# A recurrence and its feed-forward block on one core: units of single instructions, and a new order on every engine

## The chip, the cores and the metric

The kernel runs on 1 core of one Trainium2 chip. Its time is the device time of one execution, in microseconds (us). The kernel before takes 648.21 us (median of 3 runs, 648.15 to 649.47). The engines are TensorE (PE, with its weight loads as PEld), VectorE (DVE), ScalarE (ACT), GpSimd (POOL) and SyncE (SP), which issues most DMAs.

## What is computed

```python
# q, k, v, a_re, a_im: batch 4, heads 8, 768 steps, head size 48, fp32
mag = np.sqrt(a_re * a_re + a_im * a_im)
scale = np.minimum(mag, 0.999) / (mag + 1e-06)
a_re_n, a_im_n = (a_re * scale, a_im * scale)
for t in range(S):
    new_re = ar * S_re - ai * S_im
    new_im = ar * S_im + ai * S_re
    S_re, S_im = (new_re + kv, new_im)         # kv = outer product of k[t], v[t]
    y[:, :, t] = np.einsum('bhd,bhde->bhe', q[:, :, t], S_re)
x = y.transpose(0, 2, 1, 3).reshape(3072, 384)
h = np.maximum(x @ w_in, 0.0)                  # w_in 384 x 2048, given in float64
out = (h * h @ w_out).astype(np.float32)       # w_out 2048 x 384
```

## The kernel before

The sequence is cut into 24 chunks of 128 steps, and the chunks into 12 groups of 2 (`GC`). For each group a set of **operands** is made on DVE and ACT from the raw gates, queries and keys (`make_operands`, line 784): squares, an inverse root in two stages, the limit on the gates' size, products of the gates along 8-step blocks (`steps_in_blocks`, seven steps of a product and a sum), running **totals** over the blocks (`totals`, line 912, fifteen small instructions on line 918), the totals carried back into the blocks (`carries`, `carried`), and four products with queries and keys into the tile `qk`. The fourth head of each pair is copied by a DMA into the tile `last`. The first two groups (`BY_CHUNK`) are made in two halves each, chunk by chunk; the plan calls them p and q (`p0`, `q0`, `p1`, `q1`), later whole groups `o`.

Each chunk (`chunk`; `a` and `b` are the two of a group) then makes on PE its products with the state before it and its scores (both in `scores`), the transposed keys (`turns`), the values summed by the masked scores (`y`, line 1059), and the new state. `tokens` copies y into `x` on ACT, and `fill_gaps` (`g`, line 1129) fills the rest of x with two DMAs. The FFN block of a group is `first_product` (`F`, PSUM tile `h_ps`), ReLU and square on ACT (`H`), and the second product: plain for the first two groups (`T`), later with sums and differences of halves on DVE (`X`, `Y`, `Q`) that save one product in eight (`Z`, outputs `R`).

The weights arrive as 64-bit words and are decoded: two ACT instructions (`U`, `S`) and one on DVE (`A`) for each of 16 blocks. Each weight is read again later and watched on ACT (`w` loads, `W` is two ACT instructions, lines 704 and 705). At the end a range count (`K0` on DVE, `K1` one matmul, `K2` a cast) says whether the fast path held; every engine loads it (line 1456) and branches (line 1457).

No scheduler decides the order. A long string, `FRONT`, lists units in an order written out by hand, and every engine's instructions, its DMA issues too, follow that order:

```python
    by_hand = {mybir.EngineType.DVE, mybir.EngineType.PE, mybir.EngineType.SP,
               mybir.EngineType.Activation, mybir.EngineType.Pool}
    with tc.manual_schedule(engines=by_hand):
        follow(FRONT)
```

`keep_busy` (`I`) puts two filler matmuls on the identity matrix into the order (line 579, tile `idle`).

Of the kernel before, what the change touches and what calls it, by code (L numbers as in the profile page):

```python
# [33 lines left out]
P = 128  # L34
HH = 2
# [394 lines left out]
def quotient_path(ctx, tc, feat, vtok, w_in, w_out, w1, w2, out, n_seq, count):  # L430
# [77 lines left out]
    BY_CHUNK = 2  # L508

# [266 lines left out]
    def four(name="pr"):  # L776

        return tmp.tile([P, 4 * NP * D], F32, tag="pr", name=name)

    products_of = set()  # L780
# [3 lines left out]
    def make_operands(gi, only=None):  # L784
# [8 lines left out]
        tiles = {}  # L793

        def room(pool, shape, name):
            if (gi, name) not in rooms:
                rooms[gi, name] = pool.tile([P, GC // nb * shape[0], *shape[1:]], F32, name=name)
            at = 0 if only is None else only * shape[0]
            return rooms[gi, name][:, at:at + shape[0]]
# [11 lines left out]
        def steps_in_blocks(js):  # L811

            for j in js:
                ab = tiles["ab"]
                pr = four()[:, 0:4 * n].rearrange("p (k c n) -> p k c n", k=2, c=2)

                tt(pr, planes(ab[:, 2:, j - 1], -1, 0), planes(ab[:, :, j], 1, 1), ALU.mult)
                tt(ab[:, now, j], pr[:, 0], pr[:, 1], ALU.add)

        def squares():  # L820
            tiles["room"] = room(nrm, [4, E], "room")
            tiles["sq"], tiles["both"] = tiles["room"][:, 0:2], tiles["room"][:, 2:4]
            nc.scalar.activation(out=tiles["sq"], in_=r[:, A_RE:A_IM + 1], func=AF.Square)

        def real_parts():

            tiles["ab"] = room(prd, [3, L, n], "ab")
            turned(tiles["ab"][:, 1:2], r[:, A_RE:A_IM])

        def imaginary_parts():  # L830
            tiles["ab"] = room(prd, [3, L, n], "ab")
# [8 lines left out]
        def first_inverse():  # L840
            tiles["z"] = room(nrm, [1, E], "z")[:, 0]
# [9 lines left out]

        def inverse():
            u, v, z = tiles["sq"][:, 0], tiles["sq"][:, 1], tiles["z"]
            tt(v, u, v, ALU.mult)
            nc.vector.scalar_tensor_tensor(out=z, in0=v, scalar=3.0, in1=z, op0=ALU.subtract,  # L855
                                           op1=ALU.mult)


# [19 lines left out]
        def gates():  # L878
            f, low, v, ab = (tiles["both"][:, 0], tiles["both"][:, 1], tiles["sq"][:, 1],
                             tiles["ab"])  # L880
            nc.vector.scalar_tensor_tensor(out=f, in0=f, scalar=1.0, in1=low, op0=ALU.min,
                                           op1=ALU.mult)
            both_parts = ab[:, now].rearrange("p c j n -> p c (j n)")
            tt(both_parts, both_parts, f.unsqueeze(1).to_broadcast([P, 2, E]), ALU.mult)
# [605 lines left out]
```

## Time and profile before

| what | value |
|---|---|
| median of 3 runs | 648.21 us |
| the profiled execution | 651.88 us |
| its span, first to last instruction | 650.1 us |
| mean granted TensorE clock in it | 0.988 |
| PE busy | 616.5 us (95%) |
| PE weight loads busy | 554.6 us (85%) |
| DVE busy | 480.0 us (74%) |
| ACT busy | 430.5 us (66%) |
| POOL busy | 72.0 us (11%) |
| moved by DMA | 60.59 MB, mean 93 GB/s |

The shares are averages over a start, in which weights and operands have to come first, a long middle and a short end. PE's busy time counts filler matmuls too, 25.8 us of them. So the table says which engine is full on the average, and not what a change at either end of the program is worth; for that the views in order of time are needed.

### The profile page before, as it was taken

The page shows a single profiled execution, that of the slowest core. Times are in us where ns is not written, and L with a number is a line of the kernel's source. Part 1 is how long each engine was busy: PE and PEld are TensorE (multiplying, and loading weights), DVE is VectorE, ACT ScalarE, POOL GpSimd, SP SyncE. Part 2 cuts the span into 40 slices and gives each one's busy share as a digit, 9 for nine tenths or more (in the row PEclk, how much of TensorE's full clock was granted, in tenths as well). Part 3 has the DMA queues.
Part 4 walks back from the last instruction along what each step waited for, and adds up shares of the span by engine and source line. Part 5 has one row for each costly group of instructions (what it writes and reads, how often), then busy time and mean ns, then how long its engine had stood idle before and what let it go on. Part 6 is the DMA issues. An engine that isn't in the chain of part 4 may idle for free.

```text
span 650.1 us, 15843 instructions
## 1 busy us (share of the span) xinstructions
PE 616.5 (95%) x6467; PEld 554.6 (85%) x6467; DVE 480.0 (74%) x937; ACT 430.5 (66%) x847; POOL 72.0 (11%) x154
## 2 busy tenths in 40 slices
PE   2679999999999999999999999999999999999994
PEld 2678977677899889889899899999899899889994
DVE  6868887896989877977969678877957958842040
ACT  6758998667677593784686685686695584653430
POOL 7760120010100020000030010001000001000000
PEclk9879999999999999999999999999999999999998
DMA  8988575160640620722554523642541630133101
GB/s 172 178 176 182 170 234 94 40 135 11 113 80 8 123 75 8 132 64 54 112 136 117 89 44 92 114 123 77 102 99 50 93 87 13 57 86 105 49 1 31
DMA packets 41883, 60.59 MB, mean 93 GB/s; under 512 B 6024, under 2 KB 30024, under 8 KB 41800
## 3 DMA queue, kind: packets, MB, share of 16 engines
q1 hardware_dynamic: 39624, 55.46, 39.1%
q0 software_dynamic: 1888, 3.69, 3.3%
q8 instruction: 53, 0.87, 0.6%
q10 hardware_dynamic: 288, 0.32, 0.2%
q14 instruction: 30, 0.25, 0.2%
HBM read 48.76 MB, written 4.72 MB: 82 GB/s over the span
## 4 chain that ended last, share of the span: by engine, by line
PE 83%; DMA 6%; ACT 5%; DVE 2%; POOL 2%; issue 1%; ACTq 0%; POOLq 0%; DVEq 0%
PE h_ps L1153 32%; PE o_ps L1243 28%; PE o_ps L1173 5%; PE a_ps L1022 5%; PE y L1059 3%; PE h_ps L1137 3%; PE y L1005 3%; PE turns L1032 2%; PE turns L1084 2%; DMA raw<-in_feat_dram 2%; DMA words<-in_moe_w_out_dram 1%; DMA last<-qk 1%; DMA x<-x 1%; DMA words<-in_moe_w_in_dram 1%; PE idle L579 1%
## 5 line engine op out<-in xcount | busy, mean ns | idle before, releaser
L1153 PE MATMUL h_ps<-x,w 128*128 128x256 f32 x960 | 212.6, 380 | 0.0
L1153 PEld LDWEIGHTS h_ps<-x,w 128*128 128x128 f32 x960 | 180.9, 190 | 24.2 <-DMA x<-x 0.2
L1243 PE MATMUL o_ps<-w,h 128*128 128x192 f32 x640 | 110.7, 329 | 0.0
L1243 PEld LDWEIGHTS o_ps<-w,h 128*128 128x128 f32 x640 | 103.7, 190 | 1.6 <-ACT o L1116 0.3
L1160 ACT ACTIVATE h<-h_ps 128x512 f32<-128x512 f32 x80 | 47.6, 595 | 75.9 <-PE h_ps L1153 70.3
L1243 PE MATMUL o_ps<-w_sum,mix 128*128 128x192 f32 x320 | 55.9, 330 | 0.7 <-DVE o L1119 0.7
L568 POOL COPY vt<-vt 64x192 f32<-64x192 f32 x48 | 28.2, 588 | 241.2 <-DMA vt<-in_vtok_dram 229.3
L1243 PEld LDWEIGHTS o_ps<-w_sum,mix 128*128 128x128 f32 x320 | 51.7, 190 | 1.7 <-DVE o L1119 1.0
L1161 ACT ACTIVATE h<-h 128x512 f32<-128x512 f32 x80 | 50.5, 631 | 2.6
L499 DVE TENSOR_TENSOR pr<-ab 128x384 f32<-128x384 f32 (+1 forms) x98 | 49.0, 500 | 3.7 <-ACT ab L889 1.3
L499 DVE TENSOR_TENSOR mix<-h 128x256 f32<-128x256 f32 x40 | 16.9, 422 | 41.7 <-ACT h L1161 41.7
L499 DVE TENSOR_TENSOR qk<-ab,qk 128x768 f32<-128x768 f32 (+1 forms) x56 | 46.3, 844 | 1.4
L1137 PE MATMUL h_ps<-x,w 128*128 128x128 f32 x384 | 44.8, 277 | 1.5 <-DMA x<-x 1.5
L499 DVE TENSOR_TENSOR room<-ab,carry 128x1344 f32<-128x1344 f32 (+1 forms) x28 | 36.8, 1354 | 12.5 <-ACT carry L937 11.6
L1137 PEld LDWEIGHTS h_ps<-x,w 128*128 128x128 f32 x384 | 43.6, 192 | 2.5 <-issue 1.6
L1173 PE MATMUL o_ps<-w,h 128*128 128x384 f32 x128 | 44.0, 489 | 1.1 <-ACT o L1116 1.1
L1071 ACT COPY x<-y 64x256 f32<-64x256 f32 (+1 forms) x72 | 26.5, 368 | 20.0 <-PE y L1059 18.9
L808 ACT ACTIVATE ab<-raw 128x768 f32<-128x768 f32 (+1 forms) x28 | 36.8, 1371 | 2.3 <-DVE qk L499 2.3
L1022 PE MATMUL a_ps<-qk 48*64 48x64 f32 (+1 forms) x1152 | 37.6, 245 | 0.0
L579 PE MATMUL idle<-ident 128*128 128x128 f32 x168 | 25.8, 325 | 12.4 <-POOL ident masks.py:199 12.4
L808 ACT ACTIVATE room<-z 128x768 f32<-128x768 f32 (+1 forms) x27 | 36.0, 1392 | 1.6 <-DVE z L855 1.6
L1022 PEld LDWEIGHTS a_ps<-qk 48*64 48x64 f32 x1152 | 36.0, 134 | 0.7 <-issue 0.5
(114 smaller groups left out, 993.2 us busy)
## 6 DMA issues: line engine op xcount, KB each, us to landing
raw<-in_feat_dram SPq DMA_DIRECT2D x40, 288.0 KB
words<-in_moe_w_out_dram SPq DMA_DIRECT2D x8, 768.0 KB
again<-in_moe_w_in_dram SPq DMA_DIRECT2D x16, 384.0 KB
again<-in_moe_w_out_dram SPq DMA_DIRECT2D x16, 384.0 KB
last<-qk SPq DMA_DIRECT2D x48, 97.5 KB
words<-in_moe_w_in_dram SPq DMA_DIRECT2D x8, 576.0 KB
vt<-in_vtok_dram SPq DMA_DIRECT2D x48, 96.0 KB
out_dram<-o SPq DMA_DIRECT2D x23, 192.0 KB
```

Source lines behind the costliest of these rows:

```text
L499: nc.vector.tensor_tensor(out=out, in0=in0, in1=in1, op=op)
L568: nc.gpsimd.tensor_copy(out=v[half_rows(h), PAD + DM:PAD + DM + DM // 2].rearrange("t (a x) -> t a x", x=HH * D), in_=pairs[half_rows(1 - ...
L579: nc.tensor.matmul(idle, lhsT=ident, rhs=ident, start=True, stop=True)
L808: nc.scalar.activation(out=out.rearrange("p c j n -> p c n j"), func=AF.Copy, in_=in_.rearrange("p c (n j) -> p c n j", j=L), **kwargs)
L1022: nc.tensor.matmul(to[:, :, 2] if s else to[:, :, 0:2], lhsT=operand(2 + c, p_, rows(hh))[:, half_rows(s)], rhs=q_[:, :, 1] if s else q_, ...
L1071: nc.scalar.copy(out=x_of[gi][to, odd::2, b * C:(b + 1) * C], in_=tiles["y"][odd][of, 0:NP // 2])
L1137: nc.tensor.matmul(ps[:, j], lhsT=w1_blocks[:, k, g, at:at + P], rhs=x_of[i][:, g, b * C:(b + 1) * C], start=(g == 0), stop=(g == NG - 1))
L1153: nc.tensor.matmul(ps[:, j], lhsT=w1_blocks[:, k, g, at:at + P], rhs=x_of[i][:, g], start=(g == 0), stop=(g == NG - 1))
L1160: nc.scalar.activation(out=h, in_=h_ps[i, f], func=AF.Relu, scale=of_w1)
L1161: nc.scalar.activation(out=h, in_=h, func=AF.Square)
L1173: nc.tensor.matmul(o_of[i, b], lhsT=tokens_of(i, f, b)[:, j], rhs=w2[:, k], start=(k == 0), stop=(k == NFB - 1))
L1243: nc.tensor.matmul(to, lhsT=x(k)[:, j], rhs=factor(z)[:, 2 * k + j], start=(z in (0, 1, 3) and k == j == 0), stop=(k == KH // 2 - 1 and j ...
```

## The change

Units become finer: nearly each is one instruction now (a product, a sum, a copy), so that the plan can order each by itself. The tiles of half groups are laid out so that both halves share one. The totals of the first group go from POOL to DVE. A chunk's products with the state before it become a unit of their own (`sums_of_before`), apart from the scores, and a unit of two POOL memsets (`ordered`) follows them. `FRONT` is written anew for all engines, the filler matmuls are cut from 84 to 36, and the range count has another place in it.

```diff
     BY_CHUNK = 2
+    TOTALS_ON_POOL = set()
...
-    def four(name="pr"):
-
-        return tmp.tile([P, 4 * NP * D], F32, tag="pr", name=name)
+    def two(name="pr"):
+
+        return tmp.tile([P, 2 * NP * D], F32, tag="pr", name=name, bufs=2)
...
-        def steps_in_blocks(js):
-
-            for j in js:
-                ab = tiles["ab"]
-                pr = four()[:, 0:4 * n].rearrange("p (k c n) -> p k c n", k=2, c=2)
-
-                tt(pr, planes(ab[:, 2:, j - 1], -1, 0), planes(ab[:, :, j], 1, 1), ALU.mult)
-                tt(ab[:, now, j], pr[:, 0], pr[:, 1], ALU.add)
+        def step_products(j):
+
+            ab = tiles["ab"]
+            pr = tiles["pr", j] = two()[:, 0:4 * n].rearrange("p (k c n) -> p k c n", k=2, c=2)
+            tt(pr, planes(ab[:, 2:, j - 1], -1, 0), planes(ab[:, :, j], 1, 1), ALU.mult)
+
+        def step_sums(j):
+            pr = tiles["pr", j]
+            tt(tiles["ab"][:, now, j], pr[:, 0], pr[:, 1], ALU.add)
...
         def totals():
-            total = tiles["ab"][:, now, L - 1]
-            eng = nc.gpsimd if only is not None and gi == 0 else nc.vector
-            other_room = tiles["both"].rearrange("p k e -> p (k e)")
+            eng = nc.gpsimd if (gi, only) in TOTALS_ON_POOL else nc.vector
...
+        def sums_of_before():
+
+            ys = sums_here()
+            for pair in range(0, NP, 2):
+                for c in (RE, IM):
+                    for hh in range(HH):
+                        for p_ in (pair, pair + 1):
+                            nc.tensor.matmul(
+                                ys[p_ % 2][crossed(hh, p_), p_ // 2],
+                                lhsT=states[b][1 - c_seq % 2][rows(hh), c, columns(hh, PAD + p_ * D)],
+                                rhs=operand(c, p_, rows(hh)),
+                                start=(p_ < 2 and c == RE), stop=False, skip_group_check=True)
...
+        def ordered():
+
+            nc.gpsimd.memset(states[b][1 - c_seq % 2][:, :, PAD + NP * D:], 0.0)
+            nc.gpsimd.memset(v[:, 0:PAD], 0.0)
...
     FRONT = (
-        "M6 M10 M2 l0.0.0 l0.0.1 M0 j1 p0.0 p0.3 p0.4 p0.5 p0.2 j0 p0.7 i0.1.0 p0.1 p0.8 M3 M4 "
...
-        "Z11.6 K1 K2 s11.2 R11.6 s11.0 s11.1")
+        "M8 M5 l0.0.0 M2 p0.2 M10 l0.0.1 i0.1.0 M9 j1 j3 j0 i0.1.1 p0.1 p0.0 M0 p0.3 p0.4 p0.5 "
...
+        "Z11.6 R11.6 s11.1 W7 K0 K1 K2")
```

Three places of the orders follow. First ACT at the start of the program, before: `sums` is the small activation that needs the table, `room` takes the squares, `z` the first inverse, `ab` the turned copies of the gates.

```order
L590 ACT_TABLE_LOAD
L590 ACTIVATE sums<-tiny 128x1
L823 ACTIVATE room<-raw 128x768
L842 ACTIVATE z<-room 128x384
L846 ACTIVATE room,sums<-z 128x384
L808 ACTIVATE ab<-raw 128x48x8 x2
L808 ACTIVATE room<-z 128x48x8
```

And the same place of the changed kernel:

```order
L818 ACT_TABLE_LOAD
L818 ACTIVATE ab<-raw 128x48x8
L533 DMA raw<-in_feat_dram 48x2x384
L818 ACTIVATE ab<-raw 128x48x8
L832 ACTIVATE room<-raw 128x2x384
L591 ACT_TABLE_LOAD
L591 ACTIVATE sums<-tiny 128x1
L848 ACTIVATE z<-room 128x384
L852 ACTIVATE room,sums<-z 128x384
L832 ACTIVATE room<-raw 128x2x384
L818 ACTIVATE room<-z 128x48x8
L848 ACTIVATE z<-room 128x384
```

The turned copies went ahead of the squares, a second table load stands between the squares and the first inverse, and the second half's squares and first inverse stand among the first half's pieces.

Second, DVE of the changed kernel in the midst of the first group's two halves (`pr<-ab 128x192` is a step's product, `ab<-pr 128x2x48` its sum, L955 the totals, `w_58` the first weights):

```order
L683 SCALAR_TENSOR_TENSOR w_58<-words,part 128x768
L499 TENSOR_TENSOR pr<-ab 128x192
L955 TENSOR_TENSOR pr<-ab 128x96
L499 TENSOR_TENSOR ab<-pr 128x2x48
L955 TENSOR_TENSOR ab<-pr 128x24 x2
L499 TENSOR_TENSOR pr<-ab 128x192
L955 TENSOR_TENSOR pr<-ab 128x48
L499 TENSOR_TENSOR ab<-pr 128x2x48
```

Before, these totals stood on POOL (its line 918), and DVE had the steps of one half without a break; now the totals of one half alternate with the steps of the other.

Third, DVE at the end of the changed kernel (`sums`, `ends`, `sizes` and `good` are the range count; the two L1192 are the last sums of outputs):

```order
L499 TENSOR_TENSOR h<-h 128x2x128
L1192 SCALAR_TENSOR_TENSOR o<-o_ps,o 128x192 x2
L1506 TENSOR_SCALAR sums<-sums 128x14
L1506 TENSOR_SCALAR ends<-ends 128x72
L1506 TENSOR_SCALAR sizes<-sizes 128x32 x2
L1510 TENSOR_REDUCE least<-sums 128x1
L1510 TENSOR_REDUCE least<-ends 128x1
L1510 TENSOR_REDUCE least<-sizes 128x1
L1512 TENSOR_REDUCE good<-least 128x1
L1501 CAST count<-turns 1x1
```

And ACT there, whose last watch (L705, L706) writes `sizes`:

```order
L1189 ACTIVATE o<-o_ps 128x192 x3
L705 ACTIVATE size,sizes<-again 128x384
L706 ACTIVATE size,sizes<-size,bound 128x384
L1583 TENSOR_LOAD count
```

Before, the whole of the count but matmul and cast stood ahead of DVE's last two output sums, and ACT's last watch ahead of its last two output copies; now both stand behind them.

## Rows read from the trace of the kernel before

**Rows 1.** Busy time by stretch: us, PE, PEld, DVE, ACT, POOL, clock, DMA, GB/s.

```profile
53.00:640.80 587.80, 585.81 (x6172) 525.49 (x6172) 440.78 (x837) 394.30 (x774) 36.77 (x76) 1.00 0.39 87
```

**Rows 2.** PE in order of time from 53 us: start, us, what (idle before it).

```profile
53.06 5.60 PE L1137 MATMUL h_ps<-x,w 128*128 128x128 f32 x48 [1.48 <-DMA x<-x]
58.50 0.49 PE L1032 MATMUL turns<-ident,qk 128*128 128x128 f32 x3
...
61.66 2.94 PE L1137 MATMUL h_ps<-x,w 128*128 128x128 f32 x24
```

**Rows 3.** The chain that ended last, its part before 75 us: start, us, what.

```profile
17.75 0.57 POOL room L918
...
25.53 0.42 POOL ab L918 x2
...
43.80 1.21 PE y L1059 x32
...
46.54 6.39 DMA x<-x
```

**Rows 4.** ACT in order of time, at the start.

```profile
2.65 1.28 ACT L590 ACT_TABLE_LOAD   x1 [2.65 <-issue]
...
5.90 0.84 ACT L823 ACTIVATE room<-raw 128x768 f32<-128x768 f32 x1 [1.76 <-DMA raw<-in_feat_dram]
7.37 0.52 ACT L842 ACTIVATE z<-room 128x384 f32<-128x384 f32 x1 [0.62 <-DVE room L837]
...
8.44 1.52 ACT L808 ACTIVATE ab<-raw 128x384 f32<-128x384 f32 x2
```

**Rows 5.** DVE in order of time, to 71 us.

```profile
12.83 0.36 DVE L499 TENSOR_TENSOR pr<-ab 128x192 f32<-128x192 f32 x1
13.23 0.26 DVE L499 TENSOR_TENSOR ab<-pr 128x96 f32<-128x96 f32 x1
...
26.28 1.63 DVE L499 TENSOR_TENSOR room<-ab,carry 128x672 f32<-128x672 f32 x2 [1.21 <-ACT carry L937]
...
28.84 2.26 DVE L499 TENSOR_TENSOR qk<-ab,qk 128x384 f32<-128x384 f32 x4
...
38.99 0.98 DVE L682 SCALAR_TENSOR_TENSOR w<-words,part 128x768 int32<-128x768 int32 x1
39.90 0.94 DVE L499 TENSOR_TENSOR a<-a_ps,mask 128x768 f32<-128x768 f32 x1
...
67.73 0.26 DVE L918 TENSOR_TENSOR pr<-ab 128x96 f32<-128x96 f32 x1
...
70.05 0.28 DVE L918 TENSOR_TENSOR ab<-pr 128x24 f32<-128x24 f32 x2
```

**Rows 6.** ACT in order of time: copies to x, and a watch behind a reload.

```profile
45.03 1.15 ACT L1071 COPY x<-y 128x256 f32<-128x256 f32 x3 [1.31 <-PE y L1059]
...
601.44 0.56 ACT L704 ACTIVATE size<-again 128x384 bf16<-128x384 fp8e4 x1 [2.57 <-DMA again<-in_moe_w_out_dram]
```

**Rows 7.** Busy time by stretch, columns as in rows 1.

```profile
34.00:38.00 4.00, 0.37 (x5) 0.25 (x2) 3.01 (x8) 1.79 (x4) 1.27 (x3) 0.96 0.98 192
38.00:44.00 6.00, 6.00 (x53) 5.66 (x55) 3.21 (x9) 3.30 (x6) 5.35 (x16) 0.50 0.72 179
```

**Rows 8.** ACT in order of time, output copies near the end.

```profile
630.42 0.33 ACT L1116 ACTIVATE o<-o_ps 128x192 f32<-128x192 f32 x1 [3.72 <-PE o_ps L1243]
...
640.82 0.33 ACT L1116 ACTIVATE o<-o_ps 128x192 f32<-128x192 f32 x1 [7.47 <-PE o_ps L1243]
```

**Rows 9.** DVE in order of time: last reduction of the count, and its cast.

```profile
632.68 0.15 DVE L1386 TENSOR_REDUCE good<-least 128x1 f32<-128x3 f32 x1
...
640.94 0.14 DVE L1375 CAST count<-turns 1x1 int32<-1x1 f32 x1 [2.36 <-PE turns L1372]
```

**Rows 10.** Line 1457, the branch: count, ns min/median/max, first and last start.

```profile
L1457 SPq EVENT_SEMAPHORE  x8: 17/17/17, 646.1 to 646.6; - x8
...
L1457 PEldq COMPARE_BRANCH  x1: 4527/4527/4527, 641.7 to 641.7; - x1
```

More of the change, by code (lines that the diff above doesn't have):

```diff
@@ new lines, in totals, with before_blocks, at_end @@
+            steps, m = [], 1
+            while m < NB:
+                steps += [first_products] if m == 1 else [
+                    lambda m=m, k=k: part_products(m, k) for k in (RE, IM)]
+                steps += [lambda m=m: real_totals(m), lambda m=m: imaginary_totals(m)]
+                m *= 2
+            return steps
+        def before_blocks():
+            return tiles["ab"][:, now, L - 1].rearrange("p c (s n) -> p c s n", n=NB)[
+                :, :, :, 0:NB - 1]
+        def at_end():
+            return tiles["ab"][:, now, L - 1].rearrange(
+                "p c (b g n) -> p c b g n", g=NG, n=NB)[:, :, :, :, NB - 1]
@@ L948, in carried @@
             pr = tiles["room"].rearrange("p (k c) e -> p k c e", k=2)[:, :, :, 0:n * (L - 1)]
-            for k in (RE, IM):
-                tt(pr[:, k].rearrange("p c (j n) -> p c j n", n=n), planes(x[:, k:], 0),
-                   planes(w[:, 1 - k:], 1), ALU.mult)
-            tt(x.rearrange("p c j n -> p c (j n)"), pr[:, 0], pr[:, 1], ALU.add)
+            tt(pr[:, k].rearrange("p c (j n) -> p c j n", n=n), planes(x[:, k:], 0),
+               planes(w[:, 1 - k:], 1), ALU.mult)
+        def carried():
+            x = tiles["ab"][:, now, 0:L - 1]
+            pr = tiles["room"].rearrange("p (k c) e -> p k c e", k=2)[:, :, :, 0:n * (L - 1)]
+            if only is None:
+                tt(x.rearrange("p c j n -> p c (j n)"), pr[:, 0], pr[:, 1], ALU.add)
+                return
+            sides = [pr[:, k].rearrange("p c (j n) -> p c j n", n=n) for k in range(2)]
+            tt(x, sides[0], sides[1], ALU.add)
         def products(i):
@@ L999, in scores @@
                 :, :, 0:NP // 2 * 3 * ROWS].rearrange("s hh (a i t) -> s hh a i t", i=3, t=ROWS)
-            if not first:
-                for two in range(0, NP, 2):
-                    for c in (RE, IM):
-                        for hh in range(HH):
-                            for p_ in (two, two + 1):
-                                nc.tensor.matmul(
-                                    ys[p_ % 2][crossed(hh, p_), p_ // 2],
-                                    lhsT=states[b][1 - c_seq % 2][rows(hh), c, columns(hh, PAD + p_ * D)],
-                                    rhs=operand(c, p_, rows(hh)),
-                                    start=(p_ < 2 and c == RE), stop=False, skip_group_check=True)
             for a in range(NP // 2):
@@ L1386, in ranges @@
         nc.vector.tensor_reduce(out=good, in_=least, op=ALU.min, axis=mybir.AxisListType.X)
[L1388 removed]
+    operands_of = [make_operands(gi) for gi in range(NGR)]
     halves_of = [[make_operands(gi, b) for b in range(GC)] for gi in range(BY_CHUNK)]
```

217 lines of the change are left out of this document (125 added, 92 removed), and 221 rows, old and new, of the table FRONT.

## The prediction

> **What bounds the kernel now.** I read four views in this order: busy time by stretch, TensorE (PE) in order of time, the chain of waits at the start, and every engine at the end. From 53 us to 640.8 us PE is busy for 585.81 of 587.80 us, at a granted clock of 1.00, the upper of its two levels, 2.4 GHz [rows 1]. The change adds no matmul and removes none but fillers, so nothing it does to VectorE (DVE), ScalarE (ACT) or GpSimd (POOL) can shorten that stretch by more than the 2 us that are missing there. Time is won only before the first feed-forward (FFN) matmul at 53.06 [rows 2], or after the last matmul.
>
> Ahead of 53.06 the chain of waits runs through the first half group, chunk p: POOL's running totals from 17.75 to 25.95, 8.2 us, and much later the fill of x, a DMA of 6.39 us [rows 3]. That one is long because bulk loads are queued before it: the DMA engines are 0.98 busy from 34 to 38 us, and 0.72 after that [rows 7].
>
> **Part by part: the start.** *Later by 3.5 us.* ACT's new order puts p's two turned copies (1.52 together) in front of the squares, and a second table load (1.28) in front of the first inverse [rows 4]. Before, squares began at 5.90 and the first inverse at 7.37 [rows 4]. Now the first inverse comes at 5.90 + 1.52 + 0.84 + 1.28, and 0.2 for the small activation after the load: 9.8. From there to the first step product it took 12.83 - 7.37 = 5.46 [rows 4, 5]. Of that, 1.52 is done already, but four pieces of q stand in ACT's queue ahead of p's negation: squares 0.84, first inverse 0.52, its square, about as long, and one turn, 0.76 [rows 4], together 2.6. So p's first product starts at 9.8 + 5.46 - 1.52 + 2.6, about 16.3, not 12.83.
>
> *Gained on POOL.* The totals now run on DVE. Where DVE does the same fifteen instructions for a later half group it takes 70.33 - 67.73 = 2.6 us [rows 5], against 8.2. But DVE now does p and q together. Up to p's last product its queue holds: fourteen steps at 0.36 + 0.26, 8.7; two sets of totals, 5.2; three decodes at 0.98, 2.9; five pieces of 384 elements at 0.57 (a quarter of 2.26), 2.8; q's two-plane scaling and two scans at 0.94 to 0.98, 2.9; p's carried products and sum, 28.84 - 26.28 = 2.6; p's four products, 2.3 [rows 5]. That is 27.4. A consumer starts 0.04 after its producer ends (13.23 after 12.83 + 0.36), a neighbour that doesn't wait starts 0.07 before (39.90 after 38.99 + 0.98) [rows 5]; some 75 instructions, mostly alternating between p and q, save about 0.05 each: 23.5. p is ready at 16.3 + 23.5 = 39.8 (at the latest 43.7), well after the 31.10 of before. q then needs its carried part, one decode, its four products and one more small piece, 2.6 + 0.98 + 2.3 + 0.6, less the overlap 5.8: 45.6.
>
> *From there to the first FFN matmul.* The mask multiply of the first scores is next on DVE, 0.94 [rows 5]: 46.5. PE's 32 value matmuls take 1.21 [rows 3], the three copies to x 1.15 [rows 6]: 49.1 with the gaps. Then two small DMAs fill x's gaps. I bound them by 2.57, which a reload took when the queues were quiet [rows 6], and by 6.39 behind bulk [rows 3]. In SP's new order they stand ahead of the next weight loads, and the raw loads before them wait only for copies that ACT makes before p is ready, so I take 3.2, near the quiet end. The first FFN tile starts at 52.3. Its weights are there: after the mask multiply DVE has two decodes and four small pieces, 2.0 + 2.3, to 50.8.
>
> *Work moved ahead of it.* Before, the first FFN tiles were followed by chunk b's key transposes, scores and eight filler records, 61.66 - 58.50 = 3.16, and later by three transposes more, about 0.4 [rows 2]. These now stand before the first tile, in time in which PE waits anyway. So 3.6 us leave the dense stretch, and the start gains 53.06 - 52.3 + 3.6 = **4.4**.
>
> *Nothing for the rest.* ACT's queue holds about 11 us of pieces between the x copies and the first tile's ReLU, which ends at 60.7; the third tile wants that PSUM room at 52.3 + 2 x 2.8 (half of 5.60 [rows 2]) + 1.2 + 0.5 = 59.6. I set this 1.1 against half of the 2 us that were missing before. The memsets that order states and scores run on POOL, which is busy for 36.77 of 587.80 us [rows 1]; were one late, the values behind it on PE would be late by as much. Single-instruction units change no duration. I take zero for the dense stretch, from -2 (all that is missing) to +3 (three decodes that PE has to wait for).
>
> **Part by part: the end.** The order shows the range count behind the last output copy and behind one more watch on ACT; sizes, four reductions, one matmul and the cast wait for that. Before, the same sequence, from the start of an output copy to the end of the last reduction, took 632.83 - 630.42 = 2.41, and was done 8 us before the final copy [rows 8, 9]. From the final copy's start at 640.82 it now ends at 643.23; with 0.45 for matmul and cast (at least the 0.26 from 640.82 to the old cast's end) the count is there at 643.7, not at 641.08 [rows 8, 9]: 2.6 later. All engines load it and branch. PE's branch alone took 4.53, to 646.2; SP's last semaphore came at 646.6 [rows 10]. PE's now ends at 648.8, so the end moves by 2.2 to 2.6, or by 1.8 if SP alone counts, which loaded the count late. I take **+2.3**.
>
> **Sum.** -4.4 + 2.3 = -2.1 on the profiled execution's span of 650.1 us. That execution took 651.88, 3.7 above the median of 648.21; I carry the difference over: 646.1.
>
> **A rule against the change.** PE was busy for 0.37 of the 4 us from 34 to 38, and the granted clock was then 0.50, the lower level of 1.2 GHz, over all of 38 to 44, though PE was busy throughout [rows 7]. The new order has 36 filler matmuls, the old one 84, and PE waits some 2 us before the first values. In the Trainium skill, "TensorE: Matmul & The Clock Gate", section "HAM oscillation — how this bites in real kernels", says that a wait between bursts of matmuls drops the clock, and that the next burst pays for the rise again. By that rule, with which the trace agrees at 38 us, the sum would be that of the third rival.
>
> **Rivals.** *Late start (0.20), the slower side.* The first tile must start before 53.06 + 3.6 - 2.3 = 54.4, or the kernel loses. With half the overlap on DVE (2 us) and an x fill of 5.4, it starts at 56.5. The gain is then 53.06 + 3.6 - 56.5 = 0.2, and -0.2 + 2.3 = +2.1: 650.3. For it: DVE's queue is one long file, and every late decode stops it. Against it: few loads are ahead of the x fill.
> *No net change (0.12).* DVE and ACT can't follow when PE is ahead of them, and half of the 4.4 is given back as waits before 150 us: -2.2 + 2.3, 648.3. In the dense stretch DVE was busy for 440.78 us and ACT for 394.30 [rows 1], so on average there is room.
> *Low clock (0.10).* The first FFN tiles run at 1.2 GHz for the 6 us of rows 7 and do half their work: +3.0, 649.1.
> *Denser still (0.10).* The missing 2 us go too: 644.1.
> *The end is hidden (0.08).* If something other than the count sets the end, the 2.3 vanish: 643.8. Against it: PE's branch and SP's semaphores end within 0.4 us of each other.
> The forecast itself has 0.40.
>
> **How the numbers follow.** The predicted time is the forecast's, 646.1; its own spread is 644.3 to 648.0. The range runs from a hidden end with a start 1.3 us earlier, 642.5, to the late start with one more wait, 651.5. A measurement of this kernel tells 0.2% (1.3 us) from no change, so faster is below 646.9. Of the forecast's 0.40 about 0.30 lies there; with the denser case, the hidden end and a little of the others, 0.50. No change: the second rival, the forecast's upper part and some of the low clock, 0.24. Slower: 0.26.
>
> **What would show it.** Right: the first FFN tile near 52.3 with b's scores before it, no totals on POOL, p's products ending near 40 and q's near 46, PE ending 4 us earlier, and the cast some 2.9 us after the start of the final copy. Wrong: a first tile after 54.4, a granted clock of 0.50 behind it, waits of PE between 60 and 150 us, or a cast right behind the final copy.

## The result, and the profile after

The changed kernel takes 652.91 us (median of 8 runs, 649.85 to 655.18), the kernel before 648.18 (8 runs, 646.59 to 649.47). The ratio is 1.0071, with a 95% interval of 1.0048 to 1.0094: slower by 4.7 us, where 2.1 us less were forecast. The time lies outside the range of 642.5 to 651.5.

The changed kernel's profiled execution took 649.85 (span 648.1), the shortest of its 8 runs and 3.1 below the median; the one shown of before took 651.88, 3.7 above its median and more than any of its 8 runs. Read against each other, those two would show a gain of 2.0 us. So each kernel was profiled again: before with 646.91 (span 645.2), the change with 653.06 (span 651.3), its median. Those two differ by 6.1 us, and both pairs are needed below.

TensorE in order of time, the changed kernel's first execution (start, us, what, idle before it):

```profile
44.52 0.82 PE L1089 MATMUL a_ps<-last 48*64 48x128 f32 x3 [2.23 <-DMA last<-qk]
...
54.33 2.84 PE L1210 MATMUL h_ps<-x,w 128*128 128x128 f32 x24
57.10 0.90 PE L1132 MATMUL y<-a,vt 64*64 64x128 f32 x32
...
88.50 5.60 PE L1210 MATMUL h_ps<-x,w 128*128 128x128 f32 x48 [2.67 <-DMA x<-x]
```

The first FFN tile comes at 54.33, where [rows 2] had 53.06, and b's scores stand before it. At 88.50 there is a wait that before doesn't have: 2.67 us for the fill of x for the second group.

Its end, in order of time:

```profile
636.24 0.33 ACT L1189 ACTIVATE o<-o_ps 128x192 f32<-128x192 f32 x1 [7.47 <-PE o_ps L1318]
...
638.50 0.16 DVE L1512 TENSOR_REDUCE good<-least 128x1 f32<-128x3 f32 x1
638.71 0.19 PE L1498 MATMUL turns<-ones,good 128*1 128x1 f32 x2 [2.50 <-DVE good L1512]
638.93 0.15 DVE L1501 CAST count<-turns 1x1 int32<-1x1 f32 x1 [0.28 <-PE turns L1498]
```

The final copy starts 4.6 earlier than in [rows 8], the cast 2.7 after it instead of 0.1 [rows 9].

And now TensorE of the second execution of before:

```profile
35.74 0.32 PE L1022 MATMUL a_ps<-last 48*64 48x128 f32 x1 [0.22 <-DMA last<-qk]
...
36.94 1.95 PE L579 MATMUL idle<-ident 128*128 128x128 f32 x16
40.38 0.90 PE L1059 MATMUL y<-a,vt 64*64 64x128 f32 x32 [1.49 <-DVE a L499]
...
47.72 5.52 PE L1137 MATMUL h_ps<-x,w 128*128 128x128 f32 x48
...
87.39 10.99 PE L1137 MATMUL h_ps<-x,w 128*128 128x128 f32 x96
```

and of the second execution of the change:

```profile
53.80 2.92 PE L1210 MATMUL h_ps<-x,w 128*128 128x128 f32 x24 [0.58 <-DMA x<-x]
...
61.85 11.10 PE L1210 MATMUL h_ps<-x,w 128*128 128x128 f32 x96 [0.58 <-ACT h L1216]
...
89.63 7.22 PE L1210 MATMUL h_ps<-x,w 128*128 128x128 f32 x48 [3.53 <-DMA x<-x]
```

Before, the first tile stands at **47.72**, not at 53.06, and it waits for no fill of x. Three more profiled executions with before's start, of kernels described below, have it at 47.71 (`before_late_count`), 47.93 (`before_dve_totals`) and 47.36 (`old_start_long`); so 53.06 is the odd one. The chain of waits of the execution that the prediction was read from, and its TensorE, show where its surplus came from:

```profile
31.16 6.54 DMA last<-qk
...
46.54 6.39 DMA x<-x
```

```profile
37.75 0.73 PE L1022 MATMUL a_ps<-last 48*64 48x128 f32 x3 [3.63 <-DMA last<-qk]
...
40.18 3.62 PE L579 MATMUL idle<-ident 128*128 128x128 f32 x16
43.72 1.26 PE L1059 MATMUL y<-a,vt 64*64 64x128 f32 x32
```

Both flights were long there, and [rows 3] held the second. PE waited 3.63 for the first and 1.48 for the second [rows 2]; in the repeat these are 0.22 and nothing. Behind the first wait the 16 fillers took 3.62 at a granted clock of 0.50 [rows 7], against 1.95 in the repeat, and they stand in PE's queue ahead of the values. So the values came 3.3 later (43.72 against 40.38), though their mask multiply on DVE was only 0.5 later (39.90 [rows 5] against 39.38).

The sums of the two pairs, in us, from the first FFN tile, the final copy's start and the span:

| stretch | shown pair | repeated pair |
|---|---|---|
| start to first FFN tile | 53.06 to 54.33: +1.3 | 47.72 to 53.80: +6.1 |
| first tile to final copy | 587.76 to 581.91: -5.9 | 588.21 to 585.48: -2.7 |
| final copy to the end | 9.3 to 11.9: +2.6 | 9.3 to 12.0: +2.7 |
| span | -2.0 | +6.1 |

In the middle row, 3.6 us is work that was moved ahead of the first tile. So in the repeated pair the start loses 6.1 - 3.6 = 2.5, the end 2.7, and the stretch between loses 0.9. In the shown pair the start gains 2.3, the stretch between gains 2.3, and the end loses 2.6.

### The profile page after: what moved, and what is told of

It reads as the page before. It is cut to its first block, busy times and chain, and to the rows that moved or that the text cites. A ratio compares the mean times of both kernels' runs of the same rounds, so it can differ in the third digit from the quotient of the medians.

```text
span 648.1 us, 15691 instructions
## 1 busy us (share of the span) xinstructions
PE 599.5 (92%) x6371; PEld 541.0 (83%) x6371; DVE 471.6 (73%) x967; ACT 429.0 (66%) x848; POOL 60.1 (9%) x164
## 4 chain that ended last, share of the span: by engine, by line
PE 84%; DVE 6%; ACT 4%; DMA 3%; issue 1%; SPq 0%; POOL 0%; ACTq 0%; POOLq 0%; DVEq 0%
PE h_ps L1226 29%; PE o_ps L1318 27%; PE h_ps L1210 6%; PE a_ps L1089 5%; PE o_ps L1246 5%; PE y L1066 3%; PE y L1132 3%; PE turns L1099 2%; PE turns L1152 2%; PE idle L580 2%; DMA last<-qk 1%; DMA x<-x 1%; DMA again<-in_moe_w_out_dram 1%; DVE pr L499 1%; DVE room L499 1%
## 5 line engine op out<-in xcount | busy, mean ns | idle before, releaser
L1226 PE MATMUL h_ps<-x,w 128*128 128x256 f32 x960 | 213.7, 379 | 0.0
L1318 PE MATMUL o_ps<-w,h 128*128 128x192 f32 x640 | 109.3, 327 | 0.0
L1318 PE MATMUL o_ps<-w_sum,mix 128*128 128x192 f32 x320 | 54.9, 327 | 0.0
L1246 PE MATMUL o_ps<-w,h 128*128 128x384 f32 x128 | 43.3, 488 | 0.0
L1189 ACT ACTIVATE o<-o_ps 128x192 f32<-128x192 f32 (+1 forms) x44 | 15.0, 340 | 36.0 <-PE o_ps L1318 31.1
L569 POOL COPY vt<-vt 64x192 f32<-64x192 f32 x48 | 24.5, 510 | 154.5 <-DMA vt<-in_vtok_dram 152.2
```

Of the source, the lines that this page charges most:

```text
L569: nc.gpsimd.tensor_copy(out=v[half_rows(h), PAD + DM:PAD + DM + DM // 2].rearrange("t (a x) -> t a x", x=HH * D), in_=pairs[half_rows(1 - ...
L1226: nc.tensor.matmul(ps[:, j], lhsT=w1_blocks[:, k, g, at:at + P], rhs=x_of[i][:, g], start=(g == 0), stop=(g == NG - 1))
L1246: nc.tensor.matmul(o_of[i, b], lhsT=tokens_of(i, f, b)[:, j], rhs=w2[:, k], start=(k == 0), stop=(k == NFB - 1))
L1318: nc.tensor.matmul(to, lhsT=x(k)[:, j], rhs=factor(z)[:, 2 * k + j], start=(z in (0, 1, 3) and k == j == 0), stop=(k == KH // 2 - 1 and j ...
```

## Experiments

All were timed in five rounds beside runs of before on the same chip; before had a median of 647.91 to 648.91 in them. Theory: the loss lies at the two ends, a tail as forecast and a start that gained nothing, since before's was read from an execution in which it was late. Rivals: the clock behind the waits of the start, and new waits in the dense stretch.

### Repeats, and the range count alone

Both kernels unchanged:

> The kernel before as it is, for a second profile. Theory A (its profiled execution was late at the start, by a slow x fill or a slow copy of the last heads): median 648, a span near 646.5, and the first feed-forward tile at 49 to 51 instead of 53.06, with the stretch from there to the end as long as before, 597. Theory B (the profiled execution was slow elsewhere): first tile at 53 again, and the 3.7 us less stand behind 100 us or at the end.

> The changed kernel as it is, for a second profile and more times. Theory A (a typical run differs from the profiled one at the start): median 651.5 to 654, and where the profile's span is 2 us or more over 648.1, the added time stands before 100 us, as waits of PE for DMAs or as a longer stretch at a granted clock of 0.50. Theory B (the start is as in the first profile, and the middle varies): PE's first feed-forward tile again at 54.3, its wait at 88.5 again 2.7, and the added time stands between 100 and 636 us.

Measured: before 648.09 (ratio 0.9996, 0.9983 to 1.0009), the change 653.11 (1.0074, 1.0047 to 1.0101).

The count's place alone, once in each kernel (`after_early_count`, then `before_late_count`):

```diff
-        "... N11.2 Z11.4 R11.4 Z11.5 R11.5 s11.2 s11.0 Z11.6 R11.6 s11.1 W7 K0 K1 K2"
+        "... N11.2 W7 K0 Z11.4 R11.4 Z11.5 R11.5 s11.2 s11.0 Z11.6 K1 K2 R11.6 s11.1"
```

```diff
-        "... Z11.3 W30 K0 Z11.4 Q11.0 R11.3 Z11.5 R11.4 R11.5 Z11.6 K1 K2 s11.2 R11.6 s11.0 s11.1"
+        "... Z11.3 Z11.4 Q11.0 R11.3 Z11.5 R11.4 R11.5 Z11.6 s11.2 R11.6 s11.0 s11.1 W30 K0 K1 K2"
```

> The changed kernel with the last watch and the range count ahead of the last output sums, as in the kernel before. If the end pays for the late count as the prediction has it (2.3; the two profiles show 11.9 against 9.3 us from the last full matmul to the end, 2.6): 2.3 to 2.6 us less than the changed kernel, so about 650.3, and the cast some 0.3 us behind the last matmul. If something else sets the end: within 0.5 us of the changed kernel.

> The kernel before with its last watch and the range count behind the last output copy. If the late count costs what the prediction has: 2.3 to 2.6 us more than the kernel before, about 650.6. If the end is hidden: 648.2, no change. A cost well over 3 would mean that the watch behind the last copy costs more than was thought.

Measured: the change with the early count 650.81 (1.0040, 1.0020 to 1.0060), 2.3 less; before with the late count 650.95 (1.0042, 1.0021 to 1.0063), 2.7 more. On before's side the interval leaves no room for "no change"; on the change's side the two intervals overlap, but the traces agree: from the final copy's start to the end of the span before takes 9.3, and 11.3 with the late count, the change 11.9, and 9.8 with the early one. So the tail is shown: **2.0 to 2.7 us**. What is left of the loss by the medians, 2.4 of 4.7, lies before the last matmul.

### What sets the pace of the start

Squares ahead of the turned copies (`after_squares_first`), the totals back on POOL (`after_pool_totals`), and before with its totals on DVE (`before_dve_totals`):

```diff
-        "M8 M5 l0.0.0 M2 p0.2 M10 l0.0.1 i0.1.0 M9 j1 j3 j0 i0.1.1 p0.1 p0.0 M0 p0.3 p0.4 p0.5 "
+        "M8 M5 l0.0.0 M2 M0 M10 l0.0.1 i0.1.0 M9 j1 j3 j0 i0.1.1 p0.0 p0.3 p0.4 p0.5 p0.2 p0.1 "
```

```diff
-    TOTALS_ON_POOL = set()
+    TOTALS_ON_POOL = {(0, 0), (0, 1)}
```

```diff
-            eng = nc.gpsimd if only is not None and gi == 0 else nc.vector
+            eng = nc.vector
```

> The changed kernel with the start of ACT as in the kernel before: one table load before the data, squares and first inverse ahead of the two turned copies. If the 3.5 us that the prediction gave to this order are on the path: the first step product at 13 instead of 16.5, the first feed-forward tile 2 to 3 us earlier, the kernel 2 to 3 us faster than the changed one. If the data of the second half, the decodes or the copy of the last heads hold the start: under 1 us.

> The changed kernel with the first group's totals back on POOL. If the move to DVE was worth time at the start: the first half group's products end 2 to 3 us later than 38.2, the second half's 4 us later than 44.8, and the first feed-forward tile starts at 56 to 58: 2 to 4 us more than the changed kernel. If the totals on DVE take as much from it as they give (DVE is busy for all of 20 to 40 us): within 1 us.

> The kernel before with the totals of its first group on DVE, and nothing else. If the totals on POOL hold its start, as the prediction read it from the chain of waits (8.2 us there, 2.6 on DVE): the first half's products end 1 to 3 us earlier, and the first feed-forward tile starts 1 to 3 us before 47.7; 646 to 647. If loads set the pace of its start too: within 0.7 us of 648.1, with the wait for the copy of the last heads longer by what was gained.

With the squares first the time is 654.53 (1.0095, 1.0075 to 1.0114). DVE's first step product came 3 us earlier, and ACT in order of time shows what that was worth:

```profile
18.07 1.06 ACT L667 ACTIVATE part<-words 128x768 int16<-128x768 uint32 x1 [1.60 <-DMA words<-in_moe_w_in_dram]
...
25.40 1.06 ACT L667 ACTIVATE part<-words 128x768 int16<-128x768 uint32 x1 [1.15 <-DMA words<-in_moe_w_in_dram]
...
33.99 1.09 ACT L667 ACTIVATE part<-words 128x768 int16<-128x768 uint32 x1 [2.42 <-DMA words<-in_moe_w_in_dram]
```

ACT now waits 5.2 us in all for weight words, where the changed kernel's first execution has no such wait, and PE's first tile stands at 55.04. The computing was early, the loads were not.

The totals on POOL cost about 5 us in the new order (657.77; 1.0153, 1.0138 to 1.0168). The profiled execution, 654.10, is the shortest of that kernel and shows only a part of it: DVE stood 4.47 for q's carry, PE 5.11 at 44.22, and the first tile came at 56.31. In before the same totals on DVE changed nothing (649.09; 1.0007, 0.9990 to 1.0023). DVE in order of time, p's carry and the mask multiply that the first values wait for, in before's second execution and then with the totals on DVE:

```profile
26.70 1.63 DVE L499 TENSOR_TENSOR room<-ab,carry 128x672 f32<-128x672 f32 x2 [1.20 <-ACT carry L937]
...
39.38 0.94 DVE L499 TENSOR_TENSOR a<-a_ps,mask 128x768 f32<-128x768 f32 x1
```

```profile
27.04 1.62 DVE L499 TENSOR_TENSOR room<-ab,carry 128x672 f32<-128x672 f32 x2
...
39.53 0.95 DVE L499 TENSOR_TENSOR a<-a_ps,mask 128x768 f32<-128x768 f32 x1
```

POOL's totals run beside work that DVE has to do anyway, and DVE stood for them 1.20 us (through ACT's copies into `carry`), not 8.2. With the totals in its own queue that gap is gone, but the queue is 2.6 us of work longer. The mask multiply comes at 39.53 instead of 39.38, in an execution whose first step product was 0.5 earlier, and the first tile at 47.93 instead of 47.72. So in before's order the 5.6 us that the prediction reckoned for the totals weren't worth anything: by these rows DVE itself set the pace there.

Eight more fillers in a's scores, for the clock (`after_busy_scores`):

```diff
-                if gi == 0 and b == 1 and a == 1:
-                    keep_busy(0)
-                    keep_busy(1)
+                if gi == 0 and a == 1:
+                    for i in range(2 if b else 4):
+                        keep_busy(i)
```

> The changed kernel with eight more filler matmuls inside the first chunk's scores, where PE waits 2.2 to 2.9 us for the copy of the last heads, and where the granted clock falls to 0.50 to 0.80 afterwards. If the low clock delays the first feed-forward tile: the clock stays at 1.00 from 44 to 52 us, the value products take 0.9 instead of 1.56, the first tile comes 0.5 to 1 us earlier, and the kernel is that much faster. If PE has slack there: no change within 0.5 us.

Measured: 652.58 (1.0066, 1.0046 to 1.0087), as the change. From 48 to 52 the granted clock was still 0.50, and the first tile came at 55.39. The fillers didn't raise the clock at that place, so this run doesn't price the low clock; the second execution of the change does, further down.

The raw loads of a half group moved from ahead of the first copy of last heads to behind q (`after_raw_later`):

```diff
-        "i1.2.1 V0.0 a0.1 q0.52 ...
-        "A5 A4 q0.62 I15 a0.9 ...
+        "V0.0 a0.1 q0.52 ...
+        "A5 A4 q0.62 i1.2.1 I15 a0.9 ...
```

> The changed kernel with one load moved: POOL's part of the raw data for the second group's second half goes from just ahead of the first copy of the last heads to just behind the second. Theory C (from 20 us to the first feed-forward tile the DMA engines set the pace, so what is loaded ahead of the copies counts, and not the order of the computing): the first copy of the last heads takes 4 to 5 us in flight instead of 5.9 to 7.5, PE's wait for it falls from 2.2 to 2.9 us to about 1, and the first feed-forward tile starts at 52 to 53 instead of 54; the kernel is 1 to 2 us faster than the changed one, about 651.5. Theory D (DVE's long queue sets the pace): no change of the first tile, or under 0.5 us.

Measured: 652.40 (1.0059, 1.0038 to 1.0079). PE in order of time:

```profile
52.68 2.84 PE L1210 MATMUL h_ps<-x,w 128*128 128x128 f32 x24
...
62.27 11.10 PE L1210 MATMUL h_ps<-x,w 128*128 128x128 f32 x96 [2.19 <-ACT h L1216]
...
89.31 7.10 PE L1210 MATMUL h_ps<-x,w 128*128 128x128 f32 x48 [2.80 <-DMA x<-x]
```

PE's wait for the last heads fell to 0.21, as was expected if bulk loads hold that copy up. The first tile is 1.1 to 1.7 earlier, and at 62 PE gives that back in a wait for ACT.

Before's order up to an FFN tile of the first group (`F0.2.0`) or of the second (`F1.1.0`), then the change's, both with the early count and the totals on POOL (`old_start`, `old_start_long`):

```diff
-    TOTALS_ON_POOL = set()
+    TOTALS_ON_POOL = {(0, 0), (0, 1)}
...
-        "M8 M5 l0.0.0 M2 p0.2 M10 ...
+        "M6 M10 M2 l0.0.0 l0.0.1 M0 j1 p0.0 p0.3 ...
```

> The orders of the kernel before up to its second feed-forward tile (with its totals on POOL and its fillers), the changed kernel's orders for all that is left, and the early count. If the new start is what loses: first feed-forward tile at 47.7 as in the kernel before, and 2 to 4 us less than the changed kernel with early count (650.81), so 647 to 649; the wait for the second group's x fill stays. If the rest of the new order loses as well: about 650.8, the first tile earlier and PE's waits behind it longer by as much.

> As the run with the old start, but with the old orders up to the first feed-forward tile of the second group, so that the wait for the second group's x fill (2.7 to 3.5 us in the changed kernel, and 1.6 us of lower clock behind it) is gone too. If start and fill are the losses and the middle of the new order is denser, as the profiles have it: 644 to 646.5, faster than both kernels. If the middle gains nothing: 648, as the kernel before.

Measured: 653.43 (1.0091, 1.0067 to 1.0115) and 653.42 (1.0069, 1.0049 to 1.0089). With the long one the first tile stands at 47.36, as in before, but PE then waits 3.66 at 90.65 for the fill; with the short one at 49.78, with a wait of 2.43 for a decode at 70.16. The two orders don't join, so neither run isolates the new middle; that stays open.

### The wait for the second group's fill

The issues on SyncE's queue, the changed kernel:

```profile
73.46 5.64 SPq L538 DMA_DIRECT2D raw<-in_feat_dram  x8
82.02 1.27 SPq L1202 DMA_DIRECT2D x<-x  x2
```

and the second execution of before:

```profile
84.13 1.34 SPq L1129 DMA_DIRECT2D x<-x  x2
85.58 1.04 SPq L737 DMA_DIRECT2D words<-in_moe_w_out_dram  x2
86.67 6.54 SPq L537 DMA_DIRECT2D raw<-in_feat_dram  x8
```

The third group's raw loads went from behind that fill to ahead of it. Their other half stands on POOL's queue, at 77.81 in the changed kernel (4.22 us of issuing). The fill is two DMAs of 24 KB each, and in the chain of waits of the changed kernel it took 5.66 us:

```profile
82.00 0.51 ACT h L1216
82.51 0.15 SPq L1202
82.66 0.04 issue
82.70 5.66 DMA x<-x
```

Busy time by stretch (columns as in [rows 1]) shows what it flew beside. Before, then the change, each in its second execution:

```profile
84.00:88.00 4.00, 4.00 (x48) 2.69 (x47) 3.69 (x11) 3.82 (x11) 0.00 (x0) 1.00 0.33 69
```

```profile
84.00:88.00 4.00, 2.10 (x19) 1.91 (x18) 3.27 (x17) 3.97 (x7) 0.00 (x0) 1.00 0.98 211
```

DMA engines 0.33 busy against 0.98. Three kernels ask whether the raw loads do it: moved behind the fill in the text of the order (`after_fill_first`), moved there and taken off POOL's queue (`after_one_queue`), and left out (`after_no_third_raw`):

```diff
-        "... V1.0 i2 q1.15 a1.7 a1.13 a1.4 l2 q1.20 ... q1.18 g1.0 T0.1.0 ..."
+        "... V1.0 q1.15 a1.7 a1.13 a1.4 q1.20 ... q1.18 g1.0 l2 i2 T0.1.0 ..."
```

```diff
-    TWO_QUEUES = 3
+    TWO_QUEUES = 2
...
-        "... V1.0 i2 q1.15 a1.7 a1.13 a1.4 l2 q1.20 ... q1.18 g1.0 T0.1.0 ..."
+        "... V1.0 q1.15 a1.7 a1.13 a1.4 q1.20 ... q1.18 g1.0 l2 T0.1.0 ..."
```

```diff
-        "... V1.0 i2 q1.15 a1.7 a1.13 a1.4 l2 q1.20 ..."
+        "... V1.0 q1.15 a1.7 a1.13 a1.4 q1.20 ..."
```

> The changed kernel with the fill of x for the second group issued ahead of the third group's raw loads, on SP and on POOL. If these loads make the fill slow (5.7 to 6.5 us in flight in three profiles, with PE idle for 2.7 to 3.5 us behind it and the next feed-forward tiles at a lower clock, 7.22 instead of 5.60 us): the fill takes 2.5 to 3.5 us, the wait is under 1 us, and the kernel takes 649 to 650, 3 to 4 us less than the changed kernel. If the fill is slow for another reason, or the raw loads become late in their place: within 1 us of the changed kernel, with a new wait near 95 to 100 us.

> The changed kernel with all of the third group's raw loads on SP's queue, behind the fill of x for the second group; POOL, which issued its half of them ahead of the fill, issues none. Theory E (this bulk ahead of the fill is what makes PE wait at 88 us): the fill is in flight for 3 to 3.5 us, PE's wait there is under 0.5, the next tiles take 5.60 again; 2.5 to 4 us less than the changed kernel, about 649.5. Theory F (the fill has too little work beside it on PE, whatever is loaded, or what is moved back is late in its own place): the wait falls by less than 1.5, or new waits near 95 to 115 us give it back; 652 to 653.

> The changed kernel without the third group's raw loads (it computes that group from what the second left there, so part of its output is another): 1.2 MB less ahead of and beside the fill of x at 82 us. Theory E: the wait at 88 us is gone, 3 to 5 us less than the changed kernel, 648 to 650. Theory F: the wait stays above 1.5 us, under 1.5 us less, and the loss at 88 us belongs to the order of PE's work.

*Behind the fill in the text:* 652.89 (1.0070, 1.0052 to 1.0088), no change. POOL's queue, whose other work doesn't depend on the fill, still issued its half from 79.78 to 84.05, around the fill's issue at 83.32. PE still waited, 1.62 at 88.75; the trace names a small copy of ACT's as what ended that, so this run alone doesn't convict the loads. In "DMA: Bandwidth & Descriptors", section "Issuing engines are not separate DMA queues", the Trainium skill says that DMAs of different issuers run on the same engines and interleave. The trace of the changed kernel agrees: SyncE's fill flies from 82.70 to 88.36, beside loads that POOL issued from 77.81 to 82.03 and that landed 7.1 us (median) after their issue.

*Left out:* 648.55 (0.9982, 0.9966 to 0.9997), less than the change by 4.4 by the medians and by 5.8 by the ratios. TensorE in order of time has no wait at that place:

```profile
84.78 8.37 PE L1210 MATMUL h_ps<-x,w 128*128 128x128 f32 x72
```

*One queue, behind the fill:* 655.08 (1.0094, 1.0078 to 1.0110). The wait is gone here as well, but TensorE in order of time has another:

```profile
83.34 8.36 PE L1210 MATMUL h_ps<-x,w 128*128 128x128 f32 x72
...
99.98 5.49 PE L1210 MATMUL h_ps<-x,w 128*128 128x128 f32 x24 [3.99 <-ACT h L1216]
```

The loads that follow on SyncE's queue are weight words, and ACT, which decodes them, is what PE waits for. PE also pays behind that wait: the 24 matmuls took 5.49, where a group of 24 takes 2.84 elsewhere. So the raw loads cost 4 to 6 us, shown by leaving them out; that takes out whatever waits for them as well, so it isn't the price of the fill's wait alone. Where else they were put, PE waited all the same. Nor is it SyncE's half alone: in `old_start_long` that half stood behind the fill (86.21 against 83.68), with four of POOL's eight loads ahead of it (from 81.62), and PE waited 3.66 at a DMA share of 0.79.

Two combinations followed. `after_mended` is the one queue, the early count and the later raw loads of the start together; `after_fill_apart` has the early count and one queue, with the raw loads behind one more load of weight words (`f12 l2` in place of `f12`) and the first pieces of the next group's operands behind `b1.1`:

> The changed kernel with three of the moves together: early count, POOL's raw load of the second group behind the copies of the last heads, and the third group's raw loads on one queue behind the fill. If the losses add up (2.3 at the end, 1.5 at the first tile, 3 at the fill): 646 to 647, faster than the kernel before. If the gains before 100 us are given back as before: 650 to 651, no better than with the early count alone.

> The changed kernel with early count, the third group's raw loads on one queue behind the fill and behind weight block 12, and the first pieces of the third group on ACT and DVE moved behind the decodes that stood after them. If the bulk is only at the wrong place, and its consumers can wait: no wait at 88 us, no wait of PE on ACT near 100, 3 to 4 us less than with the early count alone, 647. If the loads of weights behind it are late in their turn: PE waits for a decode or a ReLU between 95 and 115 us, and no gain, 650 to 653.

Measured: 652.52 (1.0060, 1.0039 to 1.0081) and 657.09 (1.0143, 1.0125 to 1.0162). In the first, PE starts its first tile at 51.04 and loses 7.1 us in two waits for ACT, at 61.30 and 101.00. In the second it waits 3.14 at 104.86 for last heads and 3.93 at 116.75 for a decode.

### Filling the hole of the start, and covering the wait

From 48 to 52 the changed kernel's DMA engines are nearly idle, as busy time by stretch shows (before's second execution, then the change's first):

```profile
48.00:52.00 4.00, 4.00 (x38) 4.00 (x38) 3.75 (x7) 3.97 (x9) 0.99 (x2) 1.00 1.04 167
```

```profile
44.00:48.00 4.00, 2.94 (x56) 2.44 (x60) 2.81 (x6) 3.09 (x7) 0.39 (x2) 0.83 0.71 102
48.00:52.00 4.00, 4.00 (x56) 3.43 (x49) 3.17 (x6) 3.30 (x8) 2.33 (x4) 0.50 0.15 43
```

On SyncE's queue the fill of x (49.41) stands ahead of the next weight words (50.89), and the queue waits for the copies to x. To fill that hole, one load of weight words was moved ahead of the fill (`after_seventh_early`, with the early count), and then the second group's first tile was covered by a second product that was ready (`after_covered`, which also moves two steps of a decode forward):

```diff
-        "... q0.59 p0.62 l1.2.1 U4 ...
-        "... q1.3 F0.2.0 q1.4 b0.6 f7 "
+        "... q0.59 p0.62 l1.2.1 f7 U4 ...
+        "... q1.3 F0.2.0 q1.4 b0.6 "
```

```diff
-        "... f13 F1.3.0 H1.3.0 A11 ... S12 U13 q1.60 T0.2.0 F1.0.0 ..."
+        "... f13 T0.2.0 F1.3.0 H1.3.0 A11 ... S12 U13 q1.60 F1.0.0 ..."
```

> The changed kernel with early count, and with the load of weight block 7 issued ahead of the second copy of the last heads instead of behind the fill of x, which holds SP's queue from 46.5 to 50 us while the DMA engines are 0.1 to 0.2 busy. If this hole in the loads is what makes the later ones collide: the share of 48 to 52 us rises to 0.7 or more, the loads of group three and the fill at 82 us move forward or apart, 1 to 3 us less than the changed kernel with early count (650.81). If buffers and decodes hold the loads anyway: within 0.7 us of it.

> The changed kernel with early count and block 7 early, and with four matmuls of the second product (1.3 us) moved from behind the second group's first tiles to ahead of them, into PE's wait for the fill; the decode that they need is moved forward on ACT and DVE. If the wait of 2.7 us is a matter of what stands beside it on PE: the wait falls to about 1.4, and the kernel takes 1 to 2 us less than with block 7 early (649.27), 647.5 to 648.3. If the decode comes no earlier, or the operands of the second group become later by as much: within 0.5 us of 649.27.

Measured: 649.27 (1.0029, 1.0011 to 1.0047) and 648.88 (1.0012, 0.9997 to 1.0026). By the ratios, the first gives about 0.7 us of the 2.6 that the early count alone leaves (1.0040); the intervals of those two overlap, so that step is not shown. Nor did the hole close: the DMA share of 48 to 52 was 0.24 instead of 0.15, the first tile stood at 54.21, and PE waited 2.70 for the second group's fill. The second brings the wait down to 0.81, as TensorE in order of time shows:

```profile
89.79 8.28 PE L1210 MATMUL h_ps<-x,w 128*128 128x128 f32 x72 [0.81 <-DMA x<-x]
```

With these few moves the change is level with before. No version that loads all its data was faster than before.

## Why the prediction was wrong

**The step that failed: "I carry the difference over".** The sum was made against an execution 3.7 us above the median, on the assumption that its surplus lay outside the terms. It lay inside them: the start's gain of 4.4 was reckoned from a first tile at 53.06, which was late by 5.3. From 47.72, near which all other executions of that start have it, the forecast's own first tile, 52.3, gives 47.72 + 3.6 - 52.3 = -1.0, a loss, and with the tail, as an estimate, 648.2 + 1.0 + 2.3 = 651.5; measured were 652.9. That -2.1 was forecast and -2.0 stands between the two shown executions is luck: the start gained 2.3 there instead of 4.4, and the stretch behind it 2.3 instead of nothing. The surplus can't be had from the flights' lengths either: [rows 3, 6] differ by 3.8 for a fill, but PE waited for that fill only 1.48. The larger part stood behind the copy of the last heads, for which the prediction has no term.

**DVE's long file: right, and the start loses by it.** p's first product was forecast for 16.3 and came at 16.59 in the changed kernel's first execution; p's last product ended at 38.2 (39.8 forecast), q's at 44.8 (45.6), the mask multiply at 47.0 (46.5), the copies to x at 49.8 (49.1). In the second executions p's last product ends at 31.5 before and at 38.05 after, 6.6 later, since DVE now does q's pieces among p's; from there to the first tile it is 16.2 before and 15.8 after. The forecast had 12.5 (39.8 to 52.3) for that way.

**The first tile, 52.3: 1.5 to 2.0 too early.** What the forecast left out is the copy of the last heads. It flew for 5.96 us in the first execution and 6.73 in the second; PE waited 2.23 and 2.91 for it, and DVE's mask multiply 1.20 and 1.34 for the scores behind it. In `after_raw_later`, where PE's wait was 0.21, the first tile came at 52.68. Of the first execution, the chain of waits from the values on:

```profile
47.01 1.56 PE y L1132 x32
48.57 0.83 PE turns L1099 x3
49.40 1.49 PE a_ps L1089 x32
50.89 2.00 PE idle L580 x8
52.89 1.12 PE a_ps L1089 x32
54.02 0.48 PE turns L1099 x3
54.49 1.56 PE h_ps L1210 x14
```

The forecast put b's transposes, scores and fillers "in time in which PE waits anyway". They took 5.9 us here, at a granted clock of 0.50 from 48 to 52, the lower level, and ended last, after the fill of x; before they were 3.6, at the upper one. That is the low clock of the third rival at another place than it was put: ahead of the FFN tiles, which ran at full speed (2.84 for 24). It isn't what makes the tile late, though. In the second execution the eight fillers took 1.16, the upper level:

```profile
50.75 1.16 PE L580 MATMUL idle<-ident 128*128 128x128 f32 x8
```

There b's work did fit into PE's wait for the fill, PE waited 0.58 more, and the first tile came at 53.80, only 0.5 earlier. Five more executions with these orders ahead of the tile and fillers of 1.16 have it at 54.12 to 56.15. The late-start rival had the sign right and not the mechanism: DVE's overlap was as forecast. Its threshold of 54.4 was wrong by the same 5.3: from 47.72 it is 49.0, which even the forecast's own first tile missed.

**POOL's totals, 5.6 gained: wrong for before, right in size for the change.** They were worth nothing in before's order and about 5 in the new one. The prediction set POOL's 8.2 us against DVE's 2.6, but before, DVE stood for POOL only 1.21 us, the wait in [rows 5].

**Nothing for the dense stretch: wrong.** A fill of x was waited for at 88, for 2.67 to 3.53, and in the second execution the tile behind it took 7.22 instead of 5.60, at a granted clock of 0.76. The prediction read the moves of SyncE's and POOL's queues at the start alone; the third group's raw loads, moved ahead of the second group's fill, were in the order and were not followed. Leaving them out gave 4.4 by the medians. The limit that the prediction took for a gain, "the 2 us that are missing", was none either, since the busy time itself fell: from the first tile to the final copy PE is busy for 578.2 us instead of 585.8 in the shown pair (580.1 instead of 586.1 in the repeated one), 4.0 less (2.4 less) beyond the 3.6 of moved work. The second products, lines 1243 and 1173 before, 1318 and 1246 after, add to 3.1 less busy time (110.7, 55.9 and 44.0 became 109.3, 54.9 and 43.3), the first products of line 1153, now 1226, to 1.1 more (212.6 became 213.7); why is open, and no run isolated it.

**The tail, +2.3: right.** 2.3 and 2.7 in the two experiments, and the cast came 2.7 after the final copy's start, against 2.9 forecast.

## What to carry to other kernels

Where a profiled execution is slower than the median, look for the surplus before any sum: profile the kernel once more, and compare PE's waits and granted clock on the path. A long flight is not its own price: one of 6.39 us cost a wait of 1.48, and one of 6.54 a wait of 3.63 and slow fillers behind it. Follow every moved load on every queue to the small transfer that it now flies beside; here a 24 KB fill made PE wait for 2.67 to 3.53 us. And before an engine's time is counted as saved, ask how long anyone stood for it: here it was 1.2 of 8.2 us.

## What the runs showed of the hardware

- Two DMAs of 24 KB took 5.66 and 6.51 us beside bulk loads, at a DMA share of about 1.0. They took 6.10 in `old_start_long`, at 0.79. In the second execution of before, with a share of 0.33, PE waited for the same fill not at all.
- Behind the wait of 2.67 us at 88 the next 48 matmuls of 128 columns took 5.60, at a granted clock of 1.00 of the upper level (2.4 GHz); behind the one of 3.53 us in the other execution they took 7.22, at a mean of 0.76. In the Trainium skill, "TensorE: Matmul & The Clock Gate", section "HAM oscillation — how this bites in real kernels", a wait for DMAs between bursts of matmuls lowers the clock and the next burst pays. The trace agrees in the second case, with 1.6 us, and not in the first. In front of the same matmuls in nine other kernels, the 48 took 5.59 to 5.60 behind waits of 1.62, 1.95, 2.33, 2.70 and 3.07, but 7.10 behind one of 2.80 and 7.22 behind 3.19, 3.66 and 3.70.
- The changed kernel's 14 runs fall in two halves: seven with a mean granted clock of 0.988 to 0.990 (mean 651.6 us) and seven with 0.983 to 0.986 (mean 654.2). No execution of the second half was profiled, so where its 2.7 us lie is open; by these means, up to 1.3 us of the median's loss, an estimate, is in none of the rows shown.
- The branch at the end holds PE's sequencer for 3.38 us here, from 639.7, where [rows 10] have 4.53 from 641.7. Yet from the cast to the end of the span it is 9.17 us here and 9.16 in the execution shown of before. Within before's order the end is later where the branch is longer: branches of 4.26 (`before_late_count`), 4.43 (second execution) and 4.83 (`before_dve_totals`) have 8.64, 9.15 and 10.33 us from the cast to the end.
